# Seven half-size products for two of eight block pairs of a first layer, in five of its eight passes

## The chip, the cores and the metric

The kernel runs on one core of a Trainium2 chip. The metric is the device time of one execution in microseconds (us): the median of three runs, before 799.41 us (799.21 to 800.09).

## The reference

Attention among keys and queries of the same cluster, for 4 batches, 8 heads, 768 positions and a head size of 64, feeds a two-layer network with softplus between the layers:

```
mask = q_assign[:, :, :, None] == k_assign[:, :, None, :]
scores = np.where(mask, scale * np.matmul(q, k.transpose(0, 1, 3, 2)), -1000000000.0)
attn = softmax of scores
x = matmul(attn, v), heads side by side            # 3072 tokens x 512
h = x @ w_in                                       # 512 -> 2048
g = np.maximum(h, 0.0) + np.log1p(np.exp(-np.abs(h)))
return (g @ w_out).astype(np.float32)              # 2048 -> 512
```

The inputs are float64, the output is float32. The kernel keeps each operand as two float16 halves (high and low part) and makes a product from three matmuls: high by high, high by low, low by high.

## The kernel before, in words

The 3072 tokens go in eight **passes** of 384 (a batch has two). A pass has 24 attention tiles (8 heads, 3 tiles of 128 queries), then the first layer of its 384 tokens, then the second.

- `scores` (from line 1060): four 384-column matmuls into a tile `s` of PSUM, VectorE's row maximum `negm` (line 1098), ScalarE's exponential (1106), the split into two halves `phl` (a cast by the helper of line 289 and a subtraction, 1120), and a transposing DMA from SP into `pt` (`flip`, 308 to 312).
- `attend` (1142): 18 matmuls into the bank `mbank` (1167 to 1169). After each pair of heads VectorE divides into `x32` (1191; one buffer), the result is split into `xn` (1198 to 1205; two buffers) and flipped into a quarter of `xT` (1213; two buffers, one for each of two passes).
- `ffn1` (1223): for each of 16 blocks of 128 hidden units, 12 matmuls of 384 columns (1237 to 1239) into one of two PSUM banks `h`. `softplus` (1252): exponential and logarithm on ScalarE (1258, 1259; two buffers `fa`), minimum and maximum on VectorE (1274) into `fg` (two buffers, each for a pair of blocks), and the split of the pair into `gh` (1292 to 1299), one of eight buffers `g`.
- `ffn2` (1625): 24 groups of six 512-column matmuls per half layer and pass into `o` (1641 to 1643), for passes 0 to 5. A half reads four `g` buffers in each of three rounds and frees them in the third.
- The second layer of passes 6 and 7 is already made by seven products of half-size blocks (`seven`, `product`, 1501 to 1547); its sums are made by `add` (1372) and `parts`.

**What sets the order.** Every stream of work is a generator. `Order.run` (162) picks by `PLAN`, a string with two characters for each operation, which generator issues its next operation, so the order on every engine's queue is written out by hand; waits and rings (`Order.get`, `ring`) only say what must come first. The names in `SWAPPED` say which operations take their second engine: `cast` has ScalarE first and GpSimd second, `add` VectorE first and GpSimd second, the subtractions of `ph`'s and `gh`'s partners GpSimd first and VectorE second (`either`, 279). `FILL` puts dummy matmuls of 120 columns (`warm`, 267) ahead of the n-th operation on TensorE, all near the start.

Of the kernel before, what the change touches and what calls it, by code (L numbers as in the profile page):

```python
# [8 lines left out]
F16 = mybir.dt.float16  # L9
# [15 lines left out]
FILL = {0: 45, 2: 3, 3: 7, 6: 14, 8: 10, 13: 3, 15: 4, 16: 5, 19: 6, 21: 3, 24: 8, 25: 6, 29: 5}  # L25
# [10 lines left out]
SPLIT = (10, 11, 12, 13, 14)  # L36
WRAW = {30: 45, 31: 47}
HALVES = (0,)
SWAPPED = ('E1_0', 'S1l_1', 'S1l_3', 'S2_1', 'S2_3', 'S2h_0', 'S2l_0', 'S3l_0', 'S3l_2', 'S4_0', 'S4_2', 'S4_3', 'S4h_2', 'S4l_1', 'S4l_2', 'T1a_0', 'T1a_1', 'T1a_2', 'T1a_3', 'T1c_1', 'T1c_2', 'T1c_3', 'T1h_1', 'T1h_3', 'T1l_3', 'T2a_0', 'T2a_2', 'T2c_0', 'T2c_2', 'T2h_1', 'T2h_2', 'T2h_3', 'T2l_0', 'T2l_2', 'T2l_3', 'T3a_0', 'T3a_1', 'T3a_2', 'T3a_3', 'T3b_0', 'T3b_2', 'T3c_0', 'T3c_1', 'T3h_0', 'T3h_2', 'T3h_3', 'T3l_1', 'T3l_2', 'T3l_3', 'T4a_0', 'T4h_2', 'T4h_3', 'T4l_0', 'T4l_2', 'g0_0', 'g0_2', 'g0_4', 'g0_5', 'g0_7', 'g1_0', 'g1_3', 'g2_0', 'g2_2', 'g3_1', 'g3_3', 'g3_4', 'g3_5', 'g3_7', 'g4_2', 'g4_4', 'g4_6', 'g5_5', 'g5_7', 'g6_1', 'g6_5', 'g7_1', 'g7_2', 'g7_4', 'g7_5', 'g7_6', 'g7_7', 'gh0_0', 'gh0_2', 'gh0_7', 'gh1_0', 'gh1_1', 'gh1_4', 'gh1_5', 'gh1_6', 'gh2_2', 'gh2_3', 'gh2_4', 'gh2_5', 'gh3_1', 'gh3_2', 'gh3_3', 'gh3_4', 'gh3_5', 'gh3_6', 'gh3_7', 'gh4_0', 'gh4_1', 'gh4_2', 'gh4_3', 'gh4_4', 'gh4_5', 'gh4_7', 'gh5_0', 'gh5_1', 'gh5_2', 'gh5_3', 'gh5_4', 'gh5_6', 'gh6_0', 'gh6_2', 'gh6_3', 'gh6_6', 'gh7_0', 'gh7_2', 'gh7_3', 'gh7_5', 'k0_0', 'k10', 'k14', 'k16', 'k8', 'kT1_0_1', 'kT1_2_1', 'kh10', 'kh18', 'kh2', 'kh22', 'kh24', 'kh28', 'kh30', 'kh4', 'm16_4_0', 'm4_0_0', 'm4_0_1', 'm8_2_0', 'mw_0', 'mw_1', 'p103', 'p104', 'p108', 'p109', 'p111', 'p113', 'p115', 'p126', 'p138', 'p141', 'p142', 'p154', 'p157', 'p162', 'p165', 'p168', 'p174', 'p176', 'p182', 'p183', 'p187', 'p190', 'p191', 'p20', 'p22', 'p23', 'p26', 'p27', 'p28', 'p29', 'p30', 'p32', 'p35', 'p38', 'p39', 'p41', 'p43', 'p45', 'p46', 'p48', 'p52', 'p54', 'p61', 'p63', 'p69', 'p76', 'p84', 'p85', 'p86', 'p87', 'p89', 'p95', 'p96', 'p98', 'ph100', 'ph102', 'ph103', 'ph104', 'ph106', 'ph107', 'ph108', 'ph109', 'ph110', 'ph111', 'ph112', 'ph115', 'ph116', 'ph117', 'ph119', 'ph120', 'ph121', 'ph122', 'ph123', 'ph124', 'ph125', 'ph126', 'ph127', 'ph128', 'ph129', 'ph130', 'ph131', 'ph133', 'ph135', 'ph136', 'ph137', 'ph140', 'ph141', 'ph142', 'ph143', 'ph145', 'ph146', 'ph147', 'ph149', 'ph150', 'ph151', 'ph152', 'ph153', 'ph154', 'ph156', 'ph157', 'ph158', 'ph159', 'ph160', 'ph163', 'ph164', 'ph165', 'ph167', 'ph168', 'ph169', 'ph170', 'ph171', 'ph173', 'ph174', 'ph175', 'ph176', 'ph177', 'ph178', 'ph181', 'ph184', 'ph185', 'ph189', 'ph190', 'ph25', 'ph37', 'ph43', 'ph48', 'ph49', 'ph52', 'ph53', 'ph54', 'ph56', 'ph57', 'ph60', 'ph61', 'ph63', 'ph65', 'ph66', 'ph68', 'ph71', 'ph75', 'ph76', 'ph78', 'ph80', 'ph81', 'ph82', 'ph83', 'ph86', 'ph87', 'ph88', 'ph89', 'ph90', 'ph91', 'ph94', 'ph95', 'ph97', 'ph98', 'ph99', 'q0_0_0', 'q4_0', 'qT0_0', 'qT1_0', 'qT1_1', 'u15', 'u18', 'u22', 'u23', 'u26', 'u27', 'u31', 'u33', 'u35', 'u9', 'v10', 'v22', 'v28', 'v30', 'v4', 'v6', 'vh12', 'vh14', 'vh16', 'vh18', 'vh2', 'vh20', 'vh22', 'vh24', 'vh26', 'vh28', 'vh30', 'vh4', 'vh8', 'w14', 'w22', 'w23', 'w24', 'w27', 'w31', 'w8', 'wb10', 'wb12', 'wb13', 'wb15', 'wb16', 'wb17', 'wb18', 'wb19', 'wb2', 'wb20', 'wb21', 'wb22', 'wb23', 'wb24', 'wb25', 'wb26', 'wb27', 'wb3', 'wb31', 'wb4', 'wb7', 'wb9', 'wh0', 'wh13', 'wh15', 'wh17', 'wh18', 'wh2', 'wh21', 'wh22', 'wh29', 'wh30', 'wh5', 'wh6', 'x2_2', 'x3_0', 'x4_2', 'x5_2', 'x6_1', 'x7_1', 'x7_3', 'xh0_0', 'xh0_2', 'xh1_0', 'xh1_1', 'xh1_2', 'xh1_3', 'xh2_1', 'xh2_2', 'xh3_0', 'xh4_1', 'xh4_2', 'xh5_1', 'xh5_2', 'xh6_0', 'xh6_1', 'xh6_2', 'xh6_3', 'xh7_0', 'xh7_2', 'xh7_3', 'zk12', 'zk14', 'zk16', 'zk2', 'zk22', 'zk26', 'zk28', 'zk30', 'zk4', 'zk6', 'zk8', 'zq0_0_1', 'zq0_1', 'zq12_3', 'zq16_4', 'zq24_6', 'zq24_7', 'zq28_6', 'zq28_7', 'zq4_1', 'zq8_2', 'zq8_3')
# [29 lines left out]
    "cz5bfq5bd0545bfq0q570pd057595257frfp525f5d0qfr5b565d5hd05fcz5ffr5h525d5jcz0qfp5f5d5h5h5jfs5l5l5b585a5jft5fft"
    "cz5n5h5cft5d5l5p5n5e5h5e5e5l5jd05jft0q5f5e5n5p5p5ecz5r0qd05r5l0q5p0r5r5jfrfu0q5efu5p5l5n5g5t0rd05i0q5td05e0q"  # L70
# [105 lines left out]
def tile_cluster_attention__then__softplus_ffn(  # L176
# [1543 lines left out]
```

## Time and profile before

| what | value |
|---|---|
| median of 3 runs | 799.41 us |
| the profiled execution | 799.78 us |
| its span, first to last instruction | 798.0 us |
| TensorE busy | 783.2 us (98%) |
| VectorE / ScalarE / GpSimd busy | 630.1 / 453.0 / 636.2 us |
| TensorE's granted clock | 1.000 of 2.4 GHz |

The span is what the trace covers; 1.8 us of the execution lie around it. Matmuls are pipelined, so that the records overlap: a record of 326 ns does not mean one matmul in 326 ns. What a matmul costs is read from the distance between two starts. The engine names in the rows are PE (TensorE), PEld (its weight loads), DVE (VectorE), ACT (ScalarE), POOL (GpSimd) and SP (SyncE, which issues the DMAs).

### The profile page before, as it was taken

The page shows a single profiled execution, that of the slowest core. Times are in us where ns is not written, and L with a number is a line of the kernel's source. Part 1 is how long each engine was busy: PE and PEld are TensorE (multiplying, and loading weights), DVE is VectorE, ACT ScalarE, POOL GpSimd, SP SyncE. Part 2 cuts the span into 40 slices and gives each one's busy share as a digit, 9 for nine tenths or more (in the row PEclk, how much of TensorE's full clock was granted, in tenths as well). Part 3 has the DMA queues.
Part 4 walks back from the last instruction along what each step waited for, and adds up shares of the span by engine and source line. Part 5 has one row for each costly group of instructions (what it writes and reads, how often), then busy time and mean ns, then how long its engine had stood idle before and what let it go on. Part 6 is the DMA issues. An engine that isn't in the chain of part 4 may idle for free.

```text
span 798.0 us, 19825 instructions
## 1 busy us (share of the span) xinstructions
PE 783.2 (98%) x8060; PEld 525.6 (66%) x8060; DVE 630.1 (79%) x984; ACT 453.0 (57%) x729; POOL 636.2 (80%) x520
## 2 busy tenths in 40 slices
PE   8999999899999999999999999999999999999998
PEld 7998766455666666666666666666666566676787
DVE  7999999888777878687787868676866768777796
ACT  6889999535766565355454355263454455525540
POOL 6987668548998978785789999887898998995463
PEclk9999999999999999999999999999999999999999
DMA  9997499999999999999899999999998784730101
GB/s 289 256 239 219 116 228 224 243 208 200 214 183 193 203 189 189 213 207 174 152 161 226 178 179 191 171 189 200 184 154 164 131 151 90 143 61 1 47 2 60
DMA packets 402416, 136.10 MB, mean 171 GB/s; under 512 B 379028, under 2 KB 395924, under 8 KB 402324
## 3 DMA queue, kind: packets, MB, share of 16 engines
q1 hardware_dynamic: 402324, 134.83, 86.9%
q8 instruction: 63, 1.03, 0.5%
q14 instruction: 29, 0.24, 0.1%
HBM read 35.68 MB, written 6.29 MB: 53 GB/s over the span
## 4 chain that ended last, share of the span: by engine, by line
PE 84%; DVE 7%; ACT 4%; DMA 3%; issue 1%; POOL 1%; SPq 0%; DVEq 0%; POOLq 0%; ACTq 0%
PE s L1082 12%; PE h L1237 10%; PE h L1239 10%; PE h L1238 10%; PE o L1641 7%; PE o L1643 7%; PE o L1642 7%; PE mbank L1169 3%; PE mbank L1167 3%; PE mbank L1168 3%; PE m L1519 2%; PE m L1520 2%; PE m L1518 2%; PE mbank L1163 2%; DMA wo<-in_moe_w_out_dram 1%
## 5 line engine op out<-in xcount | busy, mean ns | idle before, releaser
L1098 DVE TENSOR_REDUCE negm<-s 128x1 f32<-128x768 f32 x162 | 153.3, 951 | 77.2 <-PE s L1082 75.6
L1120 POOL TENSOR_TENSOR phl<-p,phl 128x768 f16<-128x768 f32 x115 | 201.1, 1756 | 8.9 <-DVE kn L667 3.6
L1106 ACT ACTIVATE p<-s,negm 128x768 f32<-128x768 f32 x162 | 144.9, 898 | 105.5 <-DVE negm L1098 83.4
L1237 PE MATMUL h<-xT,wi 128*128 128x384 f16 x512 | 166.7, 326 | 2.4 <-DVE fg L1274 1.9
L1239 PE MATMUL h<-xT,wi 128*128 128x384 f16 x512 | 166.9, 326 | 0.0
L1238 PE MATMUL h<-xT,wi 128*128 128x384 f16 x512 | 166.8, 326 | 0.0
L1258 ACT ACTIVATE fa<-h 128x384 f32<-128x384 f32 x128 | 62.6, 489 | 154.8 <-PE h L1239 154.3
L1082 PE MATMUL s<-kt,qt 128*128 128x384 f16 x648 | 129.7, 325 | 2.6 <-DMA qt<-n 1.2
L289 POOL CAST phl<-p 128x768 f16<-128x768 f32 x102 | 93.6, 923 | 35.8 <-ACT p L1106 25.0
L1643 PE MATMUL o<-wo,gh 128*128 128x512 f16 x288 | 109.1, 379 | 0.0
L1642 PE MATMUL o<-wo,gh 128*128 128x512 f16 x288 | 109.1, 379 | 0.0
L1641 PE MATMUL o<-wo,gh 128*128 128x512 f16 x288 | 109.1, 379 | 0.0
L1167 PE MATMUL mbank<-vb,pt 128*128 128x65 f16 x1032 | 108.4, 192 | 0.2 <-DMA pt<-phl 0.2
L1168 PE MATMUL mbank<-vb,pt 128*128 128x64 f16 x1032 | 108.4, 192 | 0.0
L1169 PE MATMUL mbank<-vb,pt 128*128 128x65 f16 x1032 | 108.1, 194 | 0.0
L1167 PEld LDWEIGHTS <-pt 128*128 128x128 f16 x1032 | 95.5, 98 | 10.8 <-DMA pt<-phl 0.8
L1168 PEld LDWEIGHTS <-pt 128*128 128x128 f16 x1032 | 95.0, 97 | 9.8
L1169 PEld LDWEIGHTS <-pt 128*128 128x128 f16 x1032 | 95.1, 97 | 0.0
L1082 PEld LDWEIGHTS <-qt 128*128 128x128 f16 x648 | 59.4, 97 | 41.2 <-issue 1.8
L1274 DVE SCALAR_TENSOR_TENSOR fg<-fa,h 128x384 f32<-128x384 f32 x104 | 56.1, 545 | 26.0 <-ACT fa L1259 21.6
L1238 PEld LDWEIGHTS <-wi 128*128 128x128 f16 x512 | 50.0, 98 | 33.6 <-issue 2.9
L1239 PEld LDWEIGHTS <-wi 128*128 128x128 f16 x512 | 50.0, 98 | 33.2
(320 smaller groups left out, 1690.8 us busy)
## 6 DMA issues: line engine op xcount, KB each, us to landing
wo<-in_moe_w_in_dram SPq DMA_DIRECT2D x16, 512.0 KB, 5.0
wo<-in_moe_w_out_dram SPq DMA_DIRECT2D x14, 512.0 KB, 4.3
rawk<-in_k_dram SPq DMA_DIRECT2D x15, 384.0 KB, 4.3
rawq<-in_q_dram SPq DMA_DIRECT2D x15, 384.0 KB, 4.6
rawv<-in_v_dram SPq DMA_DIRECT2D x12, 384.0 KB, 4.2
out_dram<-ot SPq DMA_DIRECT2D x18, 256.0 KB, 2.8
pt<-phl SPq DMA_TRANSPOSE x162, 4.2
rawv<-in_v_dram SPq DMA_DIRECT2D x8, 192.0 KB, 6.6
```

What stands on the lines that cost most here:

```text
L1082: nc.tensor.matmul(st[:, j, :SH], qt[:, s, i], kt[:, s, NT // 2 * j : NT // 2 * (j + 1)], start=(s == 0), stop=(s == 1),)
L1098: yield op("DVE", 950, lambda: nc.vector.tensor_reduce(negm, st[:, :, :SH], AX.XY, ALU.max, negate=True))
L1120: lambda e: e.tensor_tensor(phl[:, 1], p32, phl[:, 0], ALU.subtract),
L1167: nc.tensor.matmul(av, pt[:, 0, c], vb[:, c, D : 2 * D + 1], start=(c == 0), stop=False)
L1168: nc.tensor.matmul(av[:, :D], pt[:, 0, c], vb[:, c, :D], start=False, stop=False)
L1169: nc.tensor.matmul(av, pt[:, 1, c], vb[:, c, D : 2 * D + 1], start=False, stop=(c == NT - 1))
L1237: nc.tensor.matmul(hp, w[0], x[0], start=(c == 0), stop=False)
L1238: nc.tensor.matmul(hp, w[0], x[1], start=False, stop=False)
L1239: nc.tensor.matmul(hp, w[1], x[0], start=False, stop=(c == NP - 1))
L1641: nc.tensor.matmul(po, g[0], wo[:, f, 0, 0], start=(f == f0), stop=False)
L1642: nc.tensor.matmul(po, g[0], wo[:, f, 0, 1], start=False, stop=False)
L1643: nc.tensor.matmul(po, g[1], wo[:, f, 0, 0], start=False, stop=(f == f0 + NF // 2 - 1))
```

## The change

In passes 2 to 6 the pairs 2 and 3 (blocks 4 and 5, 6 and 7 of 16) of the first layer are no longer made by `ffn1`. The pair is a product of a 2 x 2 block matrix of weights (two halves of the 512 inputs, two blocks of 128 units) with a 2 x 2 block matrix of tokens (two halves of the inputs, two halves of 192 tokens), and `seven_of` makes it from seven products of blocks, each 6 matmuls of 192 columns, instead of eight.

- `tforms`: four sums of token blocks per pass, split in two halves each, kept in the `xT` of the next pass. The flips of the next pass wait for `tdone`, set when both pairs are done.
- `wforms`: four sums of weight blocks per pair, made once during passes 1 and 2. Three are kept in a buffer of `g`, which the pair holds until pass 6 (`held_by`, `give_back`); the fourth takes the place of one weight block, and `wback` restores that block for pass 7.
- `seven_of`: both `h` banks at once, three batches of products (3, 2 and 2), between them one eviction and two additions; two further additions at the end. `softplus` then runs on a bank and on an SBUF tile.
- The ring code learns to lend a buffer out and take it back. `PLAN` (3739 operations instead of 3563), `SWAPPED` and `FILL` are new from the start of the kernel on.

```diff
-FILL = {0: 45, 2: 3, 3: 7, 6: 14, 8: 10, 13: 3, 15: 4, 16: 5, 19: 6, 21: 3, 24: 8, 25: 6, 29: 5}
+FILL = {0: 45, 2: 3, 3: 7, 6: 14, 8: 10, 13: 3, 15: 4, 16: 6, 21: 14, 22: 3, 23: 6, 25: 3, 29: 5}
...
+STR = (2, 3, 4, 5, 6)
+QF = (2, 3)
+HOLD = (("g", 8, 6), ("g", 8, 6))
...
-        if pr == 0:
-            xkey[pi] = yield from ring("xT", 2)
...
+        if pr == 0 and pi - 1 not in STR:
+            yield from new_x(pi)
         else:
             yield wait("xT", pi)
+        if pi - 1 in STR:
+            yield wait("tdone", pi - 1)
         yield flip(
...
+    def turns(pi: int):
+        return [fp for fp, (_, _, last) in zip(QF, HOLD) if STR[0] <= pi <= last]
...
     def ffn1(pi: int, f: int):
+        if f // 2 in turns(pi):
+            return
...
+    def split_sum(key, ns, slow, to, t, c_ns, c_slow):
+        yield cast(f"{key}h", c_ns, c_slow, to[0], t)
+        yield add(f"{key}l", ns, slow, to[1], t, to[0], ALU.subtract)
+
+    def two_of(key, ns, slow, t, low, a, b, o):
+        yield add(f"{key}a", ns, slow, t, a[0], b[0], o)
+        yield add(f"{key}b", ns * 3 // 5, slow, low, a[1], b[1], o)
+        yield add(f"{key}c", ns, slow, t, t, low)
+
+    def one_of(key, ns, slow, t, a, o, rev):
+        first, second = (a[0], t) if rev else (t, a[0])
+        yield add(f"{key}a", ns, slow, t, first, second, o)
+        yield add(f"{key}c", ns, slow, t, t, a[1], ALU.add if rev else o)
+
+    def tforms(pi: int):
+        for pr in range(NP):
+            yield wait("x", pi, pr)
+        yield from new_x(pi + 1)
+        xk = yield from ring("x32", 1)
+        t = p2.tile([P, 2, HT], F32, tag="x32", name=f"tf_{pi}", bufs=1)
...
+        for m in (1, 2, 4, 3):
...
+    def seven_of(pi: int, q: int):
...
+        two = od.pair("h", 2)
...
+        def run(*parts):
+            def emit():
+                for w, x, to in parts:
+                    for c in range(2):
+                        nc.tensor.matmul(to, w[0][:, c], x[0][:, c], start=c == 0, stop=False)
+                        nc.tensor.matmul(to, w[0][:, c], x[1][:, c], start=False, stop=False)
+                        nc.tensor.matmul(to, w[1][:, c], x[0][:, c], start=False, stop=c == 1)
+            return op("PE", 495 * len(parts), emit)
...
+        yield wait("tf", pi, 2)
+        yield run(
+            (block(fp, 0, 0), quad(pi, 0, 0), b[0]),
+            (block(fp, 0, 1), quad(pi, 1, 0), a[0]),
+            (SF[fp, 2], TF[pi, 2], a[1]),
+        )
...
+        yield evict(f"u{pi}_{fp}", ("ACT", 360), ("DVE", 330), w[:, :HT], b[0])
...
+        yield both(e, ha, w[:, :HT])
+        yield wait("tf", pi, 3)
+        yield run((SF[fp, 1], TF[pi, 1], b[0]), (SF[fp, 3], TF[pi, 3], b[1]))
+        yield both(w, hb, e[:, HT:])
+        yield wait("tf", pi, 4)
+        yield run((SF[fp, 4], quad(pi, 1, 1), b[0]), (block(fp, 1, 1), TF[pi, 4], a[0]))
+        od.set(("sdone", pi, fp))
+        yield both(hb, hb, w[:, :HT])
+        yield op("DVE", 330, lambda: nc.vector.tensor_tensor(e[:, HT:], a[0], w[:, HT:], ALU.add))
+        od.set(ka)
+        od.spawn(softplus(pi, 2 * fp, hb, kb, w, wk))
+        od.spawn(softplus(pi, 2 * fp + 1, e, ek))
```

`both` is one VectorE `tensor_tensor` over 384 elements. `quad` and `block` name the token and weight blocks.

## Rows read from the trace of the kernel before

**Rows 1.** The page's part 1: span, busy us (share), instructions.

```profile
span 798.0 us, 19825 instructions
...
PE 783.2 (98%) x8060; PEld 525.6 (66%) x8060; DVE 630.1 (79%) x984; ACT 453.0 (57%) x729; POOL 636.2 (80%) x520
```

**Rows 2.** Stages: start:end us, length, busy us (x instructions) by engine, clock, DMA.

```profile
0.00:200.00 200.00, 188.48 (x2179) 141.24 (x2179) 181.38 (x337) 155.01 (x260) 144.87 (x136) 1.00 0.99 222
...
269.40:716.10 446.70, 446.70 (x4482) 278.39 (x4481) 332.45 (x493) 220.18 (x346) 387.50 (x310) 1.00 0.93 169
```

**Rows 3.** Groups of TensorE matmuls in 269.4 to 716.1 us: xcount, busy us, mean ns.

```profile
L1239 PE MATMUL h<-xT,wi 128*128 128x384 f16 x320 | 104.3, 326 | 0.0
...
L1082 PE MATMUL s<-kt,qt 128*128 128x384 f16 x446 | 89.2, 326 | 0.0
...
L1641 PE MATMUL o<-wo,gh 128*128 128x512 f16 x216 | 81.8, 379 | 0.0
...
L1167 PE MATMUL mbank<-vb,pt 128*128 128x65 f16 x708 | 74.2, 192 | 0.0
```

**Rows 4.** Timeline of TensorE, 300 to 310 us: start us, us, line, operation, tiles, shapes.

```profile
301.91 0.33 PE L1237 MATMUL h<-xT,wi 128*128 128x384 f16 x1
...
303.86 0.81 PE L1082 MATMUL s<-kt,qt 128*128 128x384 f16 x4
304.51 0.38 PE L1641 MATMUL o<-wo,gh 128*128 128x512 f16 x1
...
307.10 0.19 PE L1167 MATMUL mbank<-vb,pt 128*128 128x65 f16 x1
...
308.30 0.19 PE L1167 MATMUL mbank<-vb,pt 128*128 128x65 f16 x1
...
308.85 0.24 PE L737 MATMUL cnt<-eq_k,ones 128*128 128x192 f16 x1
308.93 0.33 PE L1237 MATMUL h<-xT,wi 128*128 128x384 f16 x1
```

**Rows 5.** The same timeline from 54.8 us: twelve 128-column matmuls, first and next after them.

```profile
54.89 0.22 PE L1017 MATMUL u<-qt,kt 128*128 128x128 f16 x1
...
55.56 0.28 PE L997 MATMUL turned<-eye,negu 128*65 128x128 f32 x1
```

**Rows 6.** Line 1237 alone, pass 3 (64 matmuls): stage, length, busy us.

```profile
354.70:444.90 90.20, 20.85 (x64) 6.26 (x64) 1.00 1.02 179
```

**Rows 7.** Groups of VectorE, GpSimd and ScalarE: xcount, busy us, mean ns, idle before.

```profile
L1297 DVE TENSOR_TENSOR gh<-fg,gh 128x768 f16<-128x768 f32 x23 | 26.5, 1154 | 1.0 <-ACT gh L289 1.0
...
L1191 DVE TENSOR_TENSOR x<-mbank,rs 128x384 f32<-128x384 f32 x32 | 17.7, 552 | 0.9
...
L1203 DVE TENSOR_TENSOR xn<-x,xn 128x384 f16<-128x384 f32 x7 | 7.5, 1068 | 0.6 <-POOL xn L289 0.6
...
L289 POOL CAST phl<-p 128x768 f16<-128x768 f32 x102 | 93.6, 923 | 35.8 <-ACT p L1106 25.0 <-DMA pt<-phl 9.9 <-ACT kn L289 0.7
L1297 POOL TENSOR_TENSOR gh<-fg,gh 128x768 f16<-128x768 f32 x29 | 50.9, 1755 | 1.1 <-ACT gh L289 0.7 <-DVE fg L1274 0.4
...
L1203 POOL TENSOR_TENSOR xn<-x,xn 128x384 f16<-128x384 f32 x25 | 25.4, 1016 | 2.5 <-ACT xn L289 2.2
...
L289 POOL CAST xn<-x 128x384 f16<-128x384 f32 x20 | 12.3, 617 | 11.6 <-DMA xT<-xn 10.5 <-DVE x L1191 1.1
...
L1258 ACT ACTIVATE fa<-h 128x384 f32<-128x384 f32 x128 | 62.6, 489 | 154.8 <-PE h L1239 154.3
L289 ACT CAST phl<-p 128x768 f16<-128x768 f32 x60 | 49.5, 826 | 6.8 <-DMA pt<-phl 6.2
```

**Rows 8.** Timeline of SyncE, 440 to 545 us: transposing DMAs from `xn` to `xT`.

```profile
439.56 4.41 SPq L311 DMA_TRANSPOSE xT<-xn  x2
...
469.92 1.23 SPq L311 DMA_TRANSPOSE xT<-xn  x1
```

**Rows 9.** Groups of weight loads on TensorE: xcount, busy us, mean ns.

```profile
L1237 PEld LDWEIGHTS <-wi 128*128 128x128 f16 x512 | 50.0, 98 | 30.9
```

More of the change, by code (lines that the diff above doesn't have):

```diff
@@ L126, in set, with get, pair, back @@
             self.pump(ch)
-    def get(self, tag, size):
-        k = self.rings.get(tag, 0)
-        self.rings[tag] = k + 1
-        self.free.setdefault(tag, list(range(size)))
-        return ("wait", ("ring", tag, k - size)) if k >= size else None, ("ring", tag, k)
+    def get(self, tag, size, hold=False):
+        used = self.rings.setdefault(tag, [])
+        size -= self.less.get(tag, 0)
+        key = ("ring", tag, self.count.get(tag, 0))
+        self.count[tag] = key[2] + 1
+        self.free.setdefault(tag, list(range(size)))
+        last = used[-size] if len(used) >= size else None
+        self.spot[key] = self.spot[last] if last else len(used)
+        if hold:
+            self.less[tag] = self.less.get(tag, 0) + 1
+        else:
+            used.append(key)
+        return last and ("wait", last), key
+    def pair(self, tag, size):
+        return [self.get(tag, size) for _ in range(2)]
+    def back(self, key, size):
+        used = self.rings[key[1]]
+        used.insert(len(used) - size + 1, key)
+        self.less[key[1]] -= 1
     def claim(self, key):
@@ L1111, in scores @@
             yield wait("wraw", t - 1)
+        if t >= T0 and "phl" in KEPT:
+            yield wait("held", "phl", KEPT["phl"])
         phlk = yield from ring("phl", 4)
-        phl = PHL[:, phlk[2] % 4]
+        phl = PHL[:, od.spot[phlk]]
         od.set(("phl", "new", t))
@@ L1228, in ffn1 @@
             yield wait("wr", NP * (f * P // WC) + c)
+        if f % 2 and f // 2 in turns(pi - 1):
+            yield wait("wback", f // 2)
         hk = yield from ring("h", 2)
@@ new lines, in held_by @@
+    def held_by(q: int):
+        tag, size, _ = HOLD[q]
+        if tag in ("pt", "phl", "p32"):
+            for t in range(T0 - 4, T0):
+                yield wait(tag, "new", t)
+        else:
+            yield wait("f1", STR[0] - 1, 2)
+        key = yield from ring(tag, size, True)
+        held[q] = key
+        if tag not in ("pt", "phl"):
+            to = p2.tile([P, 12 * P], F16, name=f"sums_{q}", **slot(key))
+        else:
+            to = (PT if tag == "pt" else PHL)[:, od.spot[key]]
+            to = flat(to)
+        to = to.rearrange("p (m s c t) -> p m s c t", m=3, s=2, c=2)
+        for m, a in enumerate((1, 2, 4)):
+            SF[QF[q], a] = [to[:, m, s] for s in range(2)]
+        SF[QF[q], 3] = block(QF[q], 1, 0)
+        od.set(("held", tag, q))
@@ new lines, in give_back, with temps @@
+    def give_back(q):
+        tag, size, last = HOLD[q]
+        yield wait("sdone", last, QF[q])
+        if tag == "phl":
+            yield wait("phl", "new", len(tiles) - 1)
+        elif tag in ("pt", "p32"):
+            yield wait("last", tag)
+        od.back(held[q], size)
+        od.set(held[q])
+        if tag in ("pt", "phl", "p32"):
+            od.set(("back", tag))
+    def temps(name):
+        k = yield from ring("fg", 2)
+        words = flat(p2.tile([P, 2, nb], F32, name=name, **slot(k)))
+        high = words[:, : 2 * P].rearrange("p (c t) -> p c t", c=2)
+        return k, high, words[:, 2 * P : 3 * P].bitcast(F16).rearrange("p (c t) -> p c t", c=2)
@@ L1577, in accs3 @@
     def accs3():
-        yield wait("last", "p32")
+        yield wait("back", "p32") if "p32" in KEPT else wait("last", "p32")
         for nm in "xyz":
@@ L1688, in tile_cluster_attention__then__softplus_ffn @@
         od.spawn(gen)
+    for j in range(len(QF)):
+        od.spawn(held_by(j))
+        od.spawn(wforms(j))
+        od.spawn(wback(j))
+        od.spawn(give_back(j))
+    for pi in STR:
+        od.spawn(free_t(pi))
+        od.spawn(tforms(pi))
+        for j in range(len(turns(pi))):
+            od.spawn(seven_of(pi, j))
     od.run()
```

290 lines of the change are left out of this document (207 added, 83 removed).

## The prediction

> **What bounds the kernel now.** I read the page's busy shares first, then the stages, then the lines of TensorE, and last the timeline for the pace of single matmuls. The page has TensorE busy for 783.2 of 798.0 us, VectorE for 79% and GpSimd for 80% [rows 1]. A busy TensorE need not be a TensorE at its pace, so the stage that holds the changed passes is counted out. It runs from the first `h` matmul of pass 2 (269.4 us) to that of pass 7 (716.1 us), 446.7 us in which TensorE shows no idle time at all and the full granted clock [rows 2]. The timeline gives the pace: twelve 384-column matmuls from 301.91 to 303.86 us are 162.5 ns each, twelve of 512 columns from 304.51 to 307.10 us are 215.8 ns each, and the 18 of one `mbank` group (64 or 65 columns) from 308.30 to 308.85 us 30.5 ns each [rows 4]. By the counts of the stage [rows 3], each line of `h` and `o` standing for three: 960 `h` and 446 `s` at 162.5 ns are 228.5 us, 648 `o` at 215.8 ns are 139.8 us, 2124 `mbank` at 30.5 ns are 64.8 us. That is 433.1 us; the smaller groups (second-layer halves and cluster sums, some 300 matmuls of 16 to 256 columns) fill the rest. So these passes last as long as TensorE's columns last. No other engine, queue or wait sets their end, and a column removed there is time removed, as long as the others still keep up. Before it, TensorE stands idle for 200 - 188.5 = 11.5 us of the first 200 us [rows 2]; those gaps belong to the order at the start.
>
> **TensorE: the ten pairs.** `turns` gives pairs 2 and 3 in each of passes 2 to 6, since both holds end with pass 6: ten pairs, and `ffn1` skips exactly their blocks. A pair now is 2 x 4 x 3 = 24 matmuls of 384 columns: 24 x 162.5 ns = 3.90 us. In its place come 7 products x 2 chunks x 3 = 42 matmuls of 192 columns. There is one matmul of that width in the rows: `cnt` starts at 308.85 and the next one at 308.93 us, 80 ns, read to 10 ns [rows 4]. The neighbours are finer: at 128 columns, each with a weight load of its own, twelve take 54.89 to 55.56 us, 55.8 ns each [rows 5]. A line through 128 and 384 columns gives 55.8 + 64 x (162.5 - 55.8) / 256 = 82.5 ns at 192. The bounds are proportion from either side: half of 162.5 is 81.3 ns, one and a half times 55.8 is 83.7 ns. I take 82.5: 42 x 82.5 ns = 3.47 us, so 0.43 us less per pair (0.38 to 0.49) and **4.35 us** less in all (3.8 to 4.9).
>
> TensorE: Matmul & The Clock Gate of the Trainium skill, section "Back-to-back issue gap", says otherwise of a stream in which each matmul has its weight load: about 81 ns at 128 columns and 131 ns at 512. A straight line between them, an estimate, would put 192 columns at 89 ns and 384 at 114 ns, and the pair would rise from 2.74 to 3.75 us, 10 us more in all. This trace, with 55.8 and 215.8 ns for those two widths [rows 4, 5], does not agree.
>
> **TensorE: the fills.** The new table has 123 warming matmuls of 120 columns for 119. At some 53 ns (the 128-column pace less 8 columns) four more are 0.2 us if they hold up real work, and nothing if they fill a wait. I take +0.2, the dear end, which is small.
>
> **The other engines in the stage.** Per pass two pairs bring 6 additions from PSUM, of 384 elements, and two shorter ones. By the 552 ns of `x<-mbank` [rows 7] that is at most 2 x (3 x 0.55 + 0.4) = 4.1 us of VectorE, and one eviction per pair of half that size on ScalarE, mostly. The token sums are 14 additions and 4 casts per pass. Of the 70 and 20 in five passes, the new list of swapped keys puts 43 additions and 12 casts on GpSimd. The nearest row is the subtraction `xn<-x,xn`, also 384 elements: 1068 ns on VectorE, 1016 ns on GpSimd; its cast takes 617 ns [rows 7]. That gives VectorE (27 x 1.07) + 5 x 4.1 = 49 us and GpSimd 43 x 1.02 + 12 x 0.62 = 51 us. In the same list 32 casts of `ph` of passes 2 to 6 and 9 of `gh` leave GpSimd for ScalarE (923 against 826 ns each), and 5 subtractions of `g` go from GpSimd to VectorE (1755 against 1154 ns) [rows 7]: GpSimd loses 37.8 + 8.8 = 47 us, VectorE gains 6, ScalarE 34 and some 6 more for its share of the new casts and evictions. Set against the stage's 332, 388 and 220 us of VectorE, GpSimd and ScalarE [rows 2], the new sums are about 387, 392 and 260 of 442 us: 88%, 89% and 59%. All fit, so I cost this work at nothing on the path, with TensorE's queue of `o`, `s` and `mbank` work as its cover. VectorE loses most of its slack, from 74% to 88%, and if it runs late the row maxima `negm` and with them the next tiles' transposes are late first. The weight sums (28 additions, 8 casts of 256 elements) lie in passes 1 and 2, and the way back (8 and 2) in pass 6; each has tens of us between its first and its last permissible moment, and I take nothing for them.
>
> **The two joints inside a pair.** The second batch of products overwrites the half bank that the eviction reads, and the third the two that the second addition reads. Between them TensorE either has `o`, `s` or `mbank` work in its queue, or it stands. The trace of before has no such joint. The nearest rows bound it: at most the 489 ns of an activation of 384 elements and the 552 ns of an addition [rows 7], 1.04 us a pair, 10.4 us in all; at least nothing, since more than half of the stage's columns are other work [rows 3]. It cannot gain. I take nothing, because the order is written out with these operations in it, and the order of before, built in the same way, stands nowhere in 446.7 us.
>
> **The rooms.** The token sums live in the next pass's `xT` until the pair 3 of this pass is done. So the four flips of the next pass wait on SP, and whatever is queued behind a waiting flip there, `pt<-phl` above all, waits too. Now a pass lasts some 90 us from its first `h` to the next one's [rows 6], the last two flips of pass 4 go out from 439.56 us, just ahead of its first `h` at 444.9, and the first flip of pass 5 at 469.92 us, 25 us behind it [rows 6, 8]. Blocks 4 to 7 of 16 are done after about half a pass, 45 us, which leaves 45 us for four flips that need about 1.2 to 2.2 us each. Two finished `xn` can stand waiting meanwhile. I take nothing; the bound above is a flip too late by its own 25 us shift in some pass, which would only show if attention ran dry. Two of the eight `g` buffers are gone from pass 1's end on: a second-layer half needs four at once, and leaves two for the next instead of four. Three rounds over a half take 12 x 6 x 215.8 ns = 15.5 us, of which the last frees buffers; two pairs of `h` fit into the first two, and attention fills what is left. Nothing taken.
>
> **The start.** The order there is a new one too. It can gain at most the 11.5 us of idle time [rows 2]; a loss of the same kind has no bound in the trace, and 1.5 us either way is my allowance, value nothing.
>
> **The sum.** -4.35 + 0.2 = -4.15 us. The profiled execution took 799.78 us, 1.8 more than its span; it would come to 795.6. The median of the runs is 799.41, 0.37 less: **795.2 us**.
>
> **Rivals.**
> (a) Part of it is lost: VectorE at 88% is late for some `negm`, or single joints show. At 0.2 us for each of ten pairs, half of the gain goes: 797.3 us. For it, VectorE's load; against it, ScalarE's and TensorE's order. Chance 0.18.
> (b) The gain is eaten in full, by those waits or by a start that is 3 to 5 us longer: about 799, within 0.2%, which is 1.6 us, about what a measurement of this kernel can tell from no change. Chance 0.10.
> (c) The joints show in full: 799.4 - 4.2 + 10.4 = 805.6 us, slower. It decides from 0.43 us of standing per pair on; below that the pair still gains. For it, two banks of `h` are all there are, and a pair takes both; against it, the stage's other columns. Chance 0.07.
> (d) The weight loads become the pace. Each of the 42 has one, and a load is in the records for 98 ns [rows 9]. If they did not overlap each other, the pair would take 42 x 98 ns = 4.12 us, 0.22 more than before, and the whole 801.6 us. Against it, 128-column matmuls with fresh loads come every 55.8 ns [rows 5]. Chance 0.03. The section named above is the rule that would bring this about.
> That fewer than ten pairs change is excluded by the diff, as said.
>
> **How the numbers follow.** The forecast has 0.62, with a range of its own of 793.4 (4.9 us saved, a start 1.1 better) to 796.8 (3.8 saved, a start 1.2 worse). Faster by over 0.2%: 0.62 + 0.18 = 0.80. Within 0.2%: 0.10. Slower: 0.07 + 0.03 = 0.10. The range takes in (a) and the better half of (b): 793.4 to 798.6, which leaves out the slower cases, half of (b), and a little of the forecast's own edge.
>
> **What would show it.** Right: TensorE's new lines have 420 matmuls of 192 columns at 82 to 83 ns from start to start, the old `h` lines 80 fewer matmuls each, TensorE has no idle time from 200 us on, and passes 2 to 6 together are 4 us shorter. Joints: idle time on TensorE before the second or third batch, released by VectorE or ScalarE. A late VectorE: idle time before `s` or `mbank`, released by `negm` or by `pt<-phl`. It is wrong if the 192-column pace is 90 ns or more, or if the stage up to 200 us has changed by more than 2 us.

## The result, and the profile after

The changed kernel takes **804.55 us** (median of 6 runs, 802.63 to 806.42) against 799.75 us for the kernel before on the same chip (799.21 to 801.28): ratio **1.0052**, 95% interval 1.0035 to 1.0069. The forecast was 795.2 us. The change makes the kernel slower by about 5 us. The profiled execution took 802.63 us, 2.85 more than that of before; it is the fastest of the six, so 1.95 of the 4.80 us between the medians are not in its trace. One execution of the first kernel of the experiments, at a granted clock of 0.876, took 1537.01 us and is left out below.

The page's part 1 and the chain that ended last, shares by engine:

```profile
span 800.8 us, 20430 instructions
...
PE 781.5 (98%) x8244; PEld 536.3 (67%) x8244; DVE 672.5 (84%) x1066; ACT 494.7 (62%) x794; POOL 669.7 (84%) x559
...
PE 71%; DVE 8%; ACT 7%; DMA 6%; issue 3%; POOL 3%; SPq 0%; DVEq 0%; POOLq 0%; ACTq 0%
```

TensorE is about as busy as in [rows 1], with 184 matmuls more, but only 71% of the chain that ended last lies on it, against 84% in the chain of the kernel before:

```profile
PE 84%; DVE 7%; ACT 4%; DMA 3%; issue 1%; POOL 1%; SPq 0%; DVEq 0%; POOLq 0%; ACTq 0%
```

The stages say where the rest went (columns as in [rows 2]):

```profile
0.00:200.00 200.00, 188.51 (x2212) 141.51 (x2213) 184.23 (x340) 161.22 (x268) 150.72 (x142) 1.00 1.00 224
200.00:300.00 100.00, 99.78 (x1070) 62.67 (x1069) 91.69 (x137) 63.28 (x98) 89.01 (x80) 1.00 1.06 191
300.00:400.00 100.00, 98.73 (x995) 63.16 (x992) 70.97 (x127) 50.62 (x82) 84.23 (x71) 1.00 1.01 185
400.00:500.00 100.00, 99.56 (x1110) 66.11 (x1108) 85.08 (x126) 66.72 (x99) 90.38 (x72) 1.00 0.98 178
500.00:650.00 150.00, 147.37 (x1518) 94.11 (x1517) 120.48 (x192) 87.81 (x136) 127.63 (x103) 1.00 0.99 177
650.00:750.00 100.00, 100.00 (x944) 69.02 (x943) 82.05 (x111) 54.44 (x96) 88.07 (x72) 1.00 0.45 76
```

The first 200 us are those of before: 188.51 against 188.48 us of TensorE [rows 2]. From 200 to 650 us TensorE now shows 450 - 445.44 = 4.6 us of idle time. In the kernel before it showed none there, and none up to 750 us:

```profile
200.00:750.00 550.00, 550.00 (x5503) 347.27 (x5502) 413.07 (x609) 284.20 (x449) 466.85 (x371) 1.00 0.90 163
```

The granted clock is 1.00 throughout, so nothing of this is the clock.

The matmuls are what was forecast. The groups of TensorE (columns as in [rows 3]), and the timeline of one pair's first batch:

```profile
L1286 PE MATMUL h<-xT,wi 128*128 128x384 f16 x432 | 140.8, 326 | 0.0
...
L1467 PE MATMUL h<-xT,wi 128*128 128x192 f16 x80 | 19.7, 246 | 0.0
...
L1467 PE MATMUL h<-xT,sums 128*128 128x192 f16 x60 | 14.8, 246 | 0.0
...
L1465 PE MATMUL h<-xT,sums 128*128 128x192 f16 x60 | 14.7, 246 | 0.5 <-DVE fw L542 0.4
```

```profile
392.04 0.25 PE L1465 MATMUL h<-xT,wi 128*128 128x192 f16 x1
...
393.53 0.19 PE L1200 MATMUL mbank<-vb,pt 128*128 128x65 f16 x1
```

Eighteen matmuls of 192 columns take 1.49 us, 82.8 ns each at this reading's 10 ns; over all 420 the distance from start to start is 81 to 83 ns, 82.4 in the mean, but for one that has a stand behind it. So the columns give, at the forecast's 82.5 ns, 240 x 162.5 - 420 x 82.5 ns = 4.35 us back, less the forecast's 0.2 for the fills. Against that stands time in which TensorE waits. I count it as **standing**: from each matmul's start to the next one's, what goes beyond the pace (the median distance) of its shape, where that is more than 20 ns. (The busy time hides some 0.15 us of each stand, because a record ends after the next start could have come.) Before, that is 18.3 us, all of it up to 200 us but for 0.2; after, 25.3 us, 6.5 of it from 200 us on. -4.15 + 7.0 = +2.85 us: the two profiled executions are accounted for. A second trace of the changed kernel, of 803.23 us, closes in the same way, with 25.9 us of standing. (The expectations below count up to 0.5 us less of it.)

What ended the waits on TensorE in the whole span (who waited, for what: us in total, times, longest):

```profile
PE mbank L1200 <- DMA pt<-phl: 3.2, 3, 1.8
PE s L1108 <- ACT p L1135: 2.4, 4, 0.9
...
PE o L1909 <- DVE ot L1932: 1.0, 1, 1.0
...
PE s L1108 <- DMA qt<-n: 0.7, 1, 0.7
...
PE h L1465 <- DVE fw L542: 0.4, 1, 0.4
```

Only the last line is a joint inside a seven-product pair: one wait of 0.4 us. By the pace two joints show in ten pairs, 0.60 us before the matmul at 406.46 us and 0.27 us before that at 395.87. The others are attention's score tiles, its value products and the second layer, work that the change doesn't touch. The largest two stands from 200 us on, on the timeline (engine by engine, around 545 and around 588 us):

```profile
542.61 1.64 POOL L1151 TENSOR_TENSOR phl<-p,phl 128x768 f16<-128x768 f32 x1
...
542.05 0.81 PE L1108 MATMUL s<-kt,qt 128*128 128x384 f16 x4
...
542.61 1.76 DVE L652 TENSOR_TENSOR eq_k<-eq_k,tab 128x192 f16<-128x192 f16 x1
544.40 0.35 DVE L654 TENSOR_REDUCE best_k<-eq_k 128x12 f16<-128x192 f16 x1
544.67 0.95 DVE L1124 TENSOR_REDUCE negm<-s 128x1 f32<-128x768 f32 x1
...
545.71 0.90 ACT L1135 ACTIVATE p<-s,negm 128x768 f32<-128x768 f32 x1 [1.20 <-DVE negm L1124]
...
546.66 0.81 PE L1108 MATMUL s<-kt,qt 128*128 128x384 f16 x4 [0.88 <-ACT p L1135]
...
586.49 2.40 DVE L530 TENSOR_TENSOR vb<-rawv,vb 128x768 f16<-128x768 f32 x1
588.81 0.68 DVE L1932 SCALAR_TENSOR_TENSOR ot<-o,ot 128x512 f32<-128x512 f32 x1
...
589.54 0.38 PE L1909 MATMUL o<-wo,gh 128*128 128x512 f16 x1 [0.96 <-DVE ot L1932]
```

At 545 the score tile of 542.05 is done at 542.86, but its row maximum is written behind the cluster index of a later batch's keys (line 652), which takes 1.76 us; the exponential follows at 545.71, and the tile that needs its PSUM bank waits until 546.66. At 588 the subtraction of V (line 530, 2.40 us) is written ahead of the output's `ot`, and the second layer waits for its bank. As I read it, in both places a piece of work that nobody needs yet stands ahead of one that TensorE needs now; the moves below test that. The new token and weight sums are in neither.

### The profile page after: what moved, and what is told of

It is laid out like the page before. It is cut to its first block, busy times and chain, and to the rows that moved or that the text cites. A ratio compares the mean times of both kernels' runs of the same rounds, so it can differ in the third digit from the quotient of the medians.

```text
span 800.8 us, 20430 instructions
## 1 busy us (share of the span) xinstructions
PE 781.5 (98%) x8244; PEld 536.3 (67%) x8244; DVE 672.5 (84%) x1066; ACT 494.7 (62%) x794; POOL 669.7 (84%) x559
## 4 chain that ended last, share of the span: by engine, by line
PE 71%; DVE 8%; ACT 7%; DMA 6%; issue 3%; POOL 3%; SPq 0%; DVEq 0%; POOLq 0%; ACTq 0%
PE s L1108 11%; PE h L1284 6%; PE h L1286 6%; PE h L1285 6%; PE o L1909 6%; PE o L1911 6%; PE o L1910 6%; PE mbank L1200 3%; PE mbank L1202 3%; DMA pt<-phl 3%; PE mbank L1201 3%; PE m L1786 2%; PE m L1788 2%; PE m L1787 2%; PE mbank L1196 2%
## 5 line engine op out<-in xcount | busy, mean ns | idle before, releaser
L1151 POOL TENSOR_TENSOR phl<-p,phl 128x768 f16<-128x768 f32 x109 | 191.2, 1763 | 13.0 <-ACT phl L315 10.9
L1124 DVE TENSOR_REDUCE negm<-s 128x1 f32<-128x768 f32 x162 | 153.0, 950 | 25.9 <-PE s L1108 24.7
L1284 PE MATMUL h<-xT,wi 128*128 128x384 f16 x432 | 140.7, 326 | 1.2 <-DVE fg L1540 1.1
L1286 PE MATMUL h<-xT,wi 128*128 128x384 f16 x432 | 140.8, 326 | 0.0
L1285 PE MATMUL h<-xT,wi 128*128 128x384 f16 x432 | 140.7, 326 | 0.0
L1524 ACT ACTIVATE fa<-h 128x384 f32<-128x384 f32 x108 | 52.5, 487 | 71.5 <-PE h L1286 69.2
L315 ACT CAST phl<-p 128x768 f16<-128x768 f32 x97 | 79.6, 828 | 16.0 <-DMA pt<-phl 15.2
L315 POOL CAST phl<-p 128x768 f16<-128x768 f32 x65 | 58.6, 910 | 10.6 <-ACT p L1135 5.9
L1151 DVE TENSOR_TENSOR phl<-p,phl 128x768 f16<-128x768 f32 x53 | 63.7, 1204 | 2.5 <-ACT phl L315 2.5
L1525 ACT ACTIVATE fa<-fa 128x384 f32<-128x384 f32 x118 | 61.6, 524 | 2.2
```

Source lines behind the costliest of these rows:

```text
L1124: yield op("DVE", 950, lambda: nc.vector.tensor_reduce(negm, st[:, :, :SH], AX.XY, ALU.max, negate=True))
L1151: lambda e: e.tensor_tensor(phl[:, 1], p32, phl[:, 0], ALU.subtract),
L1284: nc.tensor.matmul(hp, w[0], x[0], start=(c == 0), stop=False)
L1285: nc.tensor.matmul(hp, w[0], x[1], start=False, stop=False)
L1286: nc.tensor.matmul(hp, w[1], x[0], start=False, stop=(c == NP - 1))
```

## The experiments

**First question: what of the change makes TensorE stand?** Three theories: (1) the work of the sums on VectorE, GpSimd and ScalarE; (2) their waits, on the rooms in `xT` and the joints; (3) the newly written order itself. Four kernels, one chip, kernel before 801.46 us there. All four keep the order of the changed one: its `PLAN`, the engines that `SWAPPED` names, its `FILL`, and also its rooms, the buffers of `g`, `xT` and `x32` that are held for the sums whether these are made or not.

*No token sums; the products read the raw blocks.*

```diff
+            TF[pi, m] = plain(pi, m)
+            if m in (1, 3):
+                yield from quiet(two_of(key, ns, slow, t, to[1], quad(pi, 0, 1), quad(pi, 0, 0), ALU.subtract))
...
-            yield from split_sum(key, ns, slow, to, t, 510, 690)
+            yield from quiet(split_sum(key, ns, slow, to, t, 510, 690))
```

(`quiet` leaves each operation its turn in the order and issues nothing for it; `plain` names a raw block.)

> The changed kernel without the token sums: the 14 additions and 4 casts of each of passes 2 to 6 issue nothing, and the products read plain token blocks in their place. Seven products, combinations, weight sums and the order stay. Theory 1 (the sums' time on VectorE and GpSimd makes other work late) and theory 2 (the products' wait for the sums, and the next pass's flips' wait for the products): the gaps go and the 4.35 us of columns show, 795 to 797 us. Theory 3 (the new order itself is worse, whatever the sums cost): 802 to 805.

Measured: 804.41 us, ratio 1.0045 (1.0028 to 1.0063). No gain from leaving 70 additions and 20 casts out.

*The sums made in full, but read by nobody.*

```diff
+            to = [flat(t).bitcast(F16)[:, : 2 * HT].rearrange("p (c t) -> p c t", c=2)] * 2
+            TF[pi, m] = plain(pi, m)
```

> The changed kernel with the token sums made in full but written into their scratch tile and read by nobody; the products read plain token blocks. So the work of the sums is there and the waits on it are not. Theory 1 (work): 802 to 806 us, as the changed kernel. Theory 2 (waits): 795 to 797. Theory 3 (order): 802 to 806.

Measured: 804.31 us, ratio 1.0056 (1.0034 to 1.0077).

*The waits and the casts kept, the additions cut to 4 of 192 columns.*

```diff
+            if m in (1, 3):
+                a, b = few(quad(pi, 0, 1)), few(quad(pi, 0, 0))
+                yield from two_of(key, ns, slow, tt, lo, a, b, ALU.subtract)
...
+            yield cast(f"{key}h", 510, 690, full_hi, src_m[0])
```

> The changed kernel with the token sums cut to 4 of 192 columns, except the cast of the high part, which is made in full and read by the products; the low part is read from a plain block. So the waits of products on sums and of the next flips on products are there, and the work is some 4 casts of 18 operations plus short ones. Theory 1 (work): 796 to 798 us. Theory 2 (waits): 802 to 806. Theory 3 (order): 802 to 806.

Measured: 803.82 us, ratio 1.0034 (1.0017 to 1.0051).

*The new order with the old matmuls: the four blocks by eight products, no sums of tokens or weights, no additions of partial products; one copy per pair on VectorE instead.*

```diff
-        yield run(
-            (block(fp, 0, 0), quad(pi, 0, 0), b[0]),
-            (block(fp, 0, 1), quad(pi, 1, 0), a[0]),
-            (SF[fp, 2], TF[pi, 2], a[1]),
-        )
+        yield part(every[:3])
...
-        yield run((SF[fp, 1], TF[pi, 1], b[0]), (SF[fp, 3], TF[pi, 3], b[1]))
-        yield both(w, hb, e[:, HT:])
+        yield part(every[3:5])
+        yield idle_of(both(w, hb, e[:, HT:]))
```

> The order of the changed kernel with the ten pairs made by the 24 matmuls of 384 columns as before, in the same three places; no token or weight sums, no eviction, one VectorE copy per pair. TensorE's columns are those of the kernel before. Theory 3 (order): 4 us or more above the kernel before, 804 to 809. Theories 1 and 2: within 1.5 us of the kernel before, 799 to 801.

Measured: 807.05 us, ratio **1.0073** (1.0054 to 1.0092). Its stage from 500 us and its waits:

```profile
500.00:650.00 150.00, 146.53 (x1457) 90.03 (x1454) 115.30 (x171) 84.75 (x132) 111.07 (x83) 1.00 0.92 174
```

```profile
PE s L1108 <- ACT p L1135: 2.3, 4, 0.7
PE mbank L1200 <- DVE x L1224: 1.6, 2, 1.0
...
PE o L1928 <- DVE ot L1951: 1.0, 1, 1.0
```

From 200 us on this kernel does the work of the kernel before, with more of it on ScalarE and less on GpSimd, and its VectorE is no fuller (334.6 of 450 us in 200 to 650 us, 74%, as in [rows 2]). Yet TensorE shows 3.5 us of idle time between 500 and 650 us, and the kernel is 0.7% slower than before. So neither the sums' work nor their data nor the joints are needed for a loss of this size.

The stands are the same only in part. Of the five between 500 and 650 us three are those of the changed kernel at 545, 588 and 618 us: 0.89, 1.13 and 0.72 us by the pace, 1.04, 1.13 and 0.72 there. Two, 1.12 us before `mbank` and 0.43 before `h`, and one of 0.81 us at 333 us are not in the changed kernel's trace, and its stands at 348, 397 and 406 us are not in this one. (Without the token sums those at 348 and 406 are gone too; the one at 348 is missing as well from the changed kernel's second trace.) What is common to all four kernels is the order, (3), but with its engines and its rooms, which these runs don't separate from the written sequence; the next ones do. The seven products themselves do save: 807.05 - 804.41 = 2.6 us against the run without sums, of 4.35 us of columns, uncertain by more than 1 us as the runs scatter.

**Second question: is it single places of the order, or too much work, so that a stand mended here comes back there?** I looked up which pick of `PLAN` issues each operation at a stand, and moved six of them, one for each of the six stands above 0.5 us after 250 us, 4.99 us together. (The weight form of the sixth is one that the second layer made before, too.) One move, that of the row maximum at 545 us (`9n` is generator 347, a score tile; `1b` is generator 47, the keys):

```diff
-    "9e9f9hdodododo19doipd0ip9f9f9h1bdoiq1b9h9h9j9fcz9l9j9f189ld09h191b9j9j9l9l9ncz9f1b1bif1b9j9pikd09n9nirdodoir"
+    "9e9f9hdodododo19doipd0ip9f9f9h1bdoiq1b9h9h9j9fcz9l9j9f189ld09h191b9j9j9l9l9ncz9f1b9n1bif1b9j9pikd09nirdodoir"
```

> The changed kernel with six operations moved in its written order, nothing else: one second-layer group ahead of the scores at 347.7 us of the changed kernel's trace, one ahead of the value products at 396.8, the sum of a seven-product pair ahead of a normalisation on VectorE at 405.7, the maximum of a score tile ahead of the cluster index of the next keys at 545.4, the subtraction of V put behind a maximum and a rescale at 588.4, an exponential ahead of a cast of a weight form at 617.6. The six stands are 0.83, 0.67, 0.60, 1.04, 1.13 and 0.72 us, 4.99 in all. Theory 'places' (each stand is made where the order puts a late operation ahead of an urgent one, and is gone when the two change places): the kernel takes 5 us less than the changed one, 804.55 - 5.0 = 799.5 us on the chip of its comparison, ratio to before 0.998 to 1.001, and none of the six stands is in the trace. Theory 'load' (VectorE and GpSimd have too much to do beside each other, so that a stand mended in one place comes back in another): 803 to 805 us, ratio 1.004 to 1.006, with as much idle time of TensorE after 200 us as in the changed kernel, 6 to 6.5 us, in other places.

> The same six moves in the order of the changed kernel, but with the four blocks made by eight products as before and without token sums. It ran 807.05 us before the moves (ratio 1.0073). Theory 'places': 5 us less, 802 us, ratio 1.001 to 1.002, above the run with seven products by the 2.4 us that the two were apart without the moves (up to the 4.35 us of TensorE columns, now that less of the gain falls into a stand). Theory 'load': 806 to 807 us.

Measured, on one chip with the kernel before at 801.34 us: seven products **801.29 us, ratio 0.9982** (0.9964 to 1.0000), against 1.0052 without the moves, so 0.0070 x 801 = 5.6 us are back where 5.0 were expected. Eight products 803.52 us, ratio 1.0018 (1.0003 to 1.0033), against 1.0073: 4.4 us back, though of the six stands only three, 2.7 us together, were in that kernel's trace. By the intervals each of the two is uncertain by some 2 us. Work, engines, fills and rooms are the same with and without the moves, only places in `PLAN` differ: this is what shows that the places cost time. The place at 545 us in the kernel with six moves, whose score tile of 542.05 us starts at 545.74 there, 3.7 us later, and the waiting tile 2.65 us later, at 549.31 with no wait; then its stages:

```profile
545.74 0.81 PE L1108 MATMUL s<-kt,qt 128*128 128x384 f16 x4
546.66 0.96 DVE L1124 TENSOR_REDUCE negm<-s 128x1 f32<-128x768 f32 x1 [0.40 <-ACT p L1135]
547.53 0.54 DVE L652 TENSOR_TENSOR eq_k<-eq_k,tab 128x192 f16<-128x192 f16 x1
...
549.31 0.81 PE L1108 MATMUL s<-kt,qt 128*128 128x384 f16 x4
```

```profile
200.00:300.00 100.00, 96.78 (x1008) 60.11 (x1007) 92.53 (x132) 62.57 (x97) 85.44 (x77) 1.00 1.02 184
300.00:400.00 100.00, 99.38 (x1020) 63.77 (x1019) 71.90 (x129) 51.53 (x82) 85.57 (x73) 1.00 1.00 186
400.00:500.00 100.00, 99.90 (x1098) 66.18 (x1096) 84.07 (x125) 65.53 (x98) 90.72 (x72) 1.00 0.96 180
500.00:650.00 150.00, 149.88 (x1582) 96.62 (x1581) 123.39 (x196) 90.54 (x141) 133.51 (x105) 1.00 1.02 181
```

From 500 to 650 us TensorE works 149.88 of 150 us. Five of the six stands are gone; the first came back as 0.94 us, two groups later, since the tile behind it waits for the same exponentials. The 3.2 us in 200 to 300 us are, but for 0.1, two stands at 217 and 228 us that this execution has; it was the slowest of twelve (803.70). They are met again below.

**Third question: can all of it be had?** Nine more operations moved, at six places, three of these before 200 us (the expectations count the moves as eight, and fourteen in all).

> The kernel with six moves (801.29 us, ratio 0.9982), with eight more places of its own trace mended in the same way: a rescale ahead of a weight cast at 157 us, the copy of an output tile ahead of the cluster scores of keys at 161, a second-layer group ahead of the value products at 174, a weight form's low half and a rescale ahead of a score tile's low half at 217, the three operations of a reciprocal and its product ahead of a score tile's low half at 228, a second-layer group ahead of two score tiles at 356. Stands there in the trace of the kernel with six moves: 1.04, 0.52, 1.12, 1.53, 1.88 and 0.26 + 0.68 us, 7.0 in all; the two at 217 and 228 are 0.38 and nothing in the trace of the changed kernel, so that 4.0 us is what a common run has of them. Theory 'places': 4 us less, 797.3 us, ratio 0.991 to 0.995, faster than both kernels. Theory 'load': the stands that are left come back elsewhere and the time stays at 801, ratio 0.997 to 1.000.

Measured: 800.70 us, ratio 0.9996 (0.9980 to 1.0012). A miss: nothing beyond the six moves, where 4 us were expected. The timeline of VectorE and of TensorE around 163 us shows what became of one of the early ones:

```profile
161.30 0.69 DVE L456 SCALAR_TENSOR_TENSOR phl<-wo,phl 128x512 int32<-128x512 int32 x1 [1.13 <-POOL phl L404]
...
163.12 1.63 DVE L693 TENSOR_TENSOR kn<-rawk,kn 128x768 f16<-128x768 f32 x1
...
165.08 0.26 PE L763 MATMUL cnt<-eq_k,ones 128*128 128x192 f16 x1 [1.50 <-DVE eq_k L656]
```

The stand of 1.04 us at 158 us is mended, and one of 1.66 us (by pace) stands at 163. TensorE comes there earlier, but the operation that it waits for (line 656) is written behind one that waits 1.13 us for GpSimd (line 456) and one that takes 1.63 us (line 693). Up to 200 us VectorE is busy for 182.6 of 200 us. This kernel stands for 19.5 us there, the changed one for 18.8.

So ten moves after 200 us in their place, and the changed kernel once more beside it, on one chip:

> The kernel with six moves, and ten more moved operations, all of them after 200 us (at 217, 228, 231, 355 and 485 us); the moves before 200 us of the kernel with fourteen are left out, since there a stand mended at 158 us (1.04 us) came back at 163 (1.66). Theory 'places after 200 us, load before it': TensorE's idle time after 200 us, 3.9 us in the trace of the kernel with fourteen moves and 5.5 in that of the one with six, falls to about 1 us; up to 200 us it stays at that of the changed kernel, 18.5 to 20 us. The columns are 4.1 us less than before, the start 1 to 2 us more idle: ratio 0.995 to 0.998, faster than before. Theory 'load throughout': 3 us or more of idle time come back after 200 us in other places, ratio 0.999 to 1.001.

> The changed kernel once more, on the chip of the run with moves, for the two to be compared directly: by either theory 804 to 805 us and a ratio of 1.0035 to 1.007, as in its first comparison. If the ratio were 1.002 or less, the moves would have given back less than their comparison showed.

Measured, kernel before 800.58 us: ten and six moves **799.91 us, ratio 0.9985** (0.9971 to 1.0000); the changed kernel 804.67 us, ratio 1.0054 (1.0038 to 1.0069), where it was 1.0052 above. On one chip the moves give 4.8 us back. Its stages:

```profile
200.00:300.00 100.00, 98.50 (x1021) 60.96 (x1017) 90.93 (x134) 62.27 (x96) 87.43 (x79) 1.00 1.04 187
300.00:400.00 100.00, 99.63 (x1028) 64.19 (x1025) 71.18 (x128) 50.36 (x82) 86.35 (x73) 1.00 1.01 185
400.00:500.00 100.00, 100.00 (x1119) 66.21 (x1118) 84.92 (x126) 68.11 (x102) 90.19 (x72) 1.00 0.99 183
500.00:650.00 150.00, 149.89 (x1544) 95.99 (x1541) 123.09 (x194) 88.22 (x139) 133.48 (x105) 1.00 1.00 178
```

From 300 us on the order is nearly mended (0.5 us of idle time left in 350 us, 1.7 us by the pace). In 200 to 300 us 1.5 us of idle time remain, 2.6 by the pace, mostly in four small stands before `s` and `sim_q`; there VectorE is busy for 91 of 100 us and GpSimd for 87. The expectation of 1 us of standing after 200 us was missed: it is 4.4, and the time lies between what the two theories asked for. So the runs show as much: from 300 us on the places in the order make the stands; up to 200 us a stand mended in one place was seen to come back in another, with VectorE busy for over 90% of the time; in between they don't decide. Ten further moves are worth no time that shows beyond the first six. Both kernels with moves are faster than the changed one; against the kernel before they are 0.15 to 0.18% ahead, with intervals that end at no difference. I don't call that a version that beats it.

## Why the prediction was wrong

*What bounds the kernel*: right for before, and the reason why every stand counts: with TensorE at its pace from 200 us on, each 0.1 us of waiting is 0.1 us of time.

*The ten pairs*: right. 82.4 ns at 192 columns, 4.35 us of columns, the old lines 80 matmuls fewer each. The estimate of 89 ns from TensorE: Matmul & The Clock Gate of the Trainium skill, section "Back-to-back issue gap", does not hold here either: each of these matmuls has its weight load, at 82.4 ns.

*The fills*: 123 for 119 in the page's groups; too small to be seen apart.

*The joints*: 0.4 us of waiting, 0.9 by the pace, of a bound of 10.4. Right within a microsecond, and with them rival (c) falls; that its 805.6 us lies near the measured time is chance. Rival (d) falls by the pace.

*The other engines, at nothing*: right for the sums as work. Without the token sums (1.0045) or with a fiftieth of their additions (1.0034) the time is the same within the intervals as with all of them (1.0052). The loads themselves were forecast at 88, 89 and 59% of VectorE, GpSimd and ScalarE and are 82, 87 and 60% in 200 to 650 us.

*The rooms*: nothing found. No stand waits for `xT`, and ahead of the two of the six that wait for another flip (at 347.7 and 396.8 us) SP's queue has no flip of `xT` in the 15 us before.

*The start*: right, 188.51 us of TensorE for 188.48.

**The step that failed** is the ground on which the joints and the other engines' work were costed at nothing: "the order is written out with these operations in it, and the order of before, built in the same way, stands nowhere in 446.7 us". It takes the cover from the order of before, and that order is the one thing that the change replaces completely. The cover was a property of that string, not of the way in which such strings are made. The runs showed that the new order with the old matmuls, without the sums, costs 0.7%, and that six moved picks give 4.4 us of it back there and 5.6 us of the changed kernel's time. The step should have carried a term for a new order in the whole span, as it did for the start, where it had 1.5 us either way. The sign that failed with it is "no idle time from 200 us on"; neither of the two signs named for being wrong (a pace of 90 ns, a start changed by over 2 us) came, since both look elsewhere.

What would show a late VectorE was named rightly: idle time before `s` and `mbank`, released by way of `negm` and by `pt<-phl`. Rivals (a) and (b) had that mechanism, but tied to VectorE's load (88%) and sized at 2 to 4 us. A high load is not needed for a loss: with VectorE at 74% three of the six stands are there. Nor is it the usual lateness of the row maxima. From the end of a score tile to the start of its row maximum it takes, in the median between 200 and 716 us, 0.11 us before and 0.72 after, but 0.30 without the token sums, which is no faster, and 0.78 with ten and six moves, which is the fastest kernel of this order. So that lateness comes with the sums' work and costs nothing that shows; the stands are at single tiles. The margin shrinks with the order: from the end of the exponential that frees a bank to the start of the score tile that takes it, the median is 2.80 us before, 1.87 with the new order and eight products, 1.64 after and 1.51 with the moves, with under 1 us left for 22 of 135 tiles before and 43 of 134 after (each worked out tile by tile from the start and end times in the trace).

What stays open: with the places mended, seven products are 2.2 us faster than eight (801.29 against 803.52; as the runs scatter, 1 to 4), not 4.35. In the trace with ten and six moves the standing is still 5.1 us more than before: 0.9 up to 200 us, 2.5 in 200 to 300 us and 1.7 after it. With the 4.15 us of columns that makes, to 0.1 us, the 0.9 us by which this execution is longer than that of before. So it is seen where the gain is lost, but the runs don't settle what would get it back. Why the new order has these places can't be seen from here. Its written costs bear on it without proving it: the operation of line 652 stands in the code with 0.28 us at most and took 1.76, the subtraction of V on VectorE with 0.95 and took 2.40.

## What to carry to other kernels

When a change comes with a new order, price the order as a part of its own: run the new order with the old work before the gain of the new work is believed. When the engine that bounds the kernel stands, look at what was queued ahead of the operation that released it, not only at how busy the releasing engine is; a stand made by one urgent operation behind one that could wait can be mended by changing their places. A total of columns saved is a forecast only as long as the waits stay what they were.

## What the runs showed that I had not expected

The same operation of VectorE takes 0.25 or 1.76 us, by what GpSimd does beside it. The changed kernel, VectorE and GpSimd on the timeline at 519 us, to be held against the rows at 541 and 542 us above:

```profile
518.70 1.65 POOL L1151 TENSOR_TENSOR phl<-p,phl 128x768 f16<-128x768 f32 x1
520.31 1.67 POOL L1151 TENSOR_TENSOR phl<-p,phl 128x768 f16<-128x768 f32 x1
521.93 1.75 POOL L693 TENSOR_TENSOR kn<-rawk,kn 128x768 f16<-128x768 f32 x1
...
520.22 0.25 DVE L652 TENSOR_TENSOR eq_k<-eq_k,tab 128x192 f16<-128x192 f16 x1
520.51 0.35 DVE L654 TENSOR_REDUCE best_k<-eq_k 128x12 f16<-128x192 f16 x1
520.89 1.30 DVE L656 TENSOR_TENSOR eq_k<-eq_k,best_k 128x192 f16<-128x192 f16 x1
```

At 520.22 us line 652 falls into the joint between two of GpSimd's subtractions and takes 0.25 us. At 520.89 the like operation of line 656 meets the second one and ends at 522.19, 0.2 us after that has ended (521.97); the reduction between them, with one operand, takes its 0.35 us beside GpSimd undisturbed. At 542.61 line 652 starts with a GpSimd subtraction and ends at 544.37, 0.12 us after it. It is so throughout this trace: from 60 us on, lines 652 and 656 start 38 times while a GpSimd operation is under way, and each time they end after it has ended; the 14 times that none is, they take 0.24 to 0.36 us. So these operations, with both operands in SBUF, wait for the GpSimd operation under way, however short they are themselves. SBUF — State Buffer of the Trainium skill, section "Who interferes with whom", says the same: the two engines share a pair of ports to SBUF under an exclusive lock, held for the whole instruction, and a VectorE instruction with two inputs in SBUF contends with a GpSimd instruction that reads there. The trace agrees, with 0.25 against 1.76 us. An order that is written with one fixed cost for such an operation can't hold its duration, which depends on what the other engine is doing at that moment.

The standing in 200 to 300 us differs between executions of the same program: the changed kernel's first trace has no stand above 0.4 us there, its second one of 1.87 us before `mbank` at 224 us.
